# New orders and PSUM banks for a hand-planned attention and feed-forward kernel, with w1 loaded ahead of the first masks

## The chip, the cores and the metric

The kernel runs on one core of one Trainium2 chip. The metric is the device time of one execution in microseconds (us). It is given as the median over several executions, and beside it stands one execution taken with the hardware profiler, whose trace the quoted views come from.

## The reference

Attention with 16 extra keys ("beacons") that every query sees, and a causal mask behind them; its output goes through a two-layer network with the quick gelu.

```python
# q, k, v: (8, 8, 576, 64); beacon_k, beacon_v: (8, 8, 16, 64); w_in: (512, 2048); w_out: (2048, 512)
k_all = concatenate([beacon_k, k], axis=2)
v_all = concatenate([beacon_v, v], axis=2)
scores = (q @ k_all^T) / sqrt(64)
causal[:, 16:] = triu(ones((576, 576)), k=1)          # beacons are never masked
a = softmax(where(causal, -1e9, scores))
x = (a @ v_all), transposed to 4608 tokens x 512
h = x @ w_in
out = (h * sigmoid(1.702 * h)) @ w_out                # (4608, 512) float32
```

## The kernel before

**A plan written out.** The kernel first makes a list of some 1,740 operations. Each is made by `plan.op(...)` and numbered in the order of making; it knows its engine, an estimated duration and the operations that it depends on. Nothing is searched when the kernel is built: `ORDER` gives, for each engine, the numbers of its operations in the order in which the engine runs them (PE is TensorE, ACT ScalarE, DVE VectorE, POOL GpSimd, SP SyncE, Q the landing of transfers). `BANK` gives, for each PSUM tile in the order of the tiles' making, the PSUM bank (0 to 7) that it takes. `Plan.run` walks the lists and works out a planned start for each operation from the estimated durations. It then emits all operations sorted by planned start. Each engine runs its own instructions strictly in this order and waits at the head of its queue. What an operation waits for at run time is its data, and for the first operation on a PSUM tile also the last reader of the tile that had the bank before.

```python
todo = {e: [self.ops[i] for i in reversed(seq)] for e, seq in ORDER.items()}
keys = list(dict.fromkeys(o.ring for o in self.ops if o.ring is not None))
given = dict(zip(keys, BANK))
...
order.sort(key=lambda o: (o.start, o.seq))
```

**Attention.** The work comes in 16 sets, one for each half (four heads) of a batch row. Each set has two loads for k and q on GpSimd's queue (`ldqk`, line 452), turns of both on VectorE (`turn`, L519, with a small turn of the beacons' keys, L512, cast by `bk`, L508), scores on TensorE (`qk`, L586, later sets L575), exponentials on ScalarE (`exp`, L599, `E<-s`), causal masks on GpSimd (`mask`, L607, `E<-E`), and sums over keys on TensorE (`av`, L665). `av` with x = 2 gives the column sums of the exponentials (`u<-E,ones`), x = 0 and 1 the sums with v. VectorE takes the column sums' reciprocals (`z1` and `z2`, L675 to L686) and multiplies by them (`norm`, L703), which leaves x, transposed, in `xT` and frees the PSUM bank of the sums. In the later sets VectorE adds the key blocks up first (`zadd`, L625, `zs<-zs,E`), so that there are fewer products for the column sums.

**The feed-forward part.** The tokens come in ten groups. Groups 0 and 1 have 256 tokens each. For them a product `m1` (L727) takes two column blocks of w_in, ScalarE makes a tanh (L742), VectorE the gate (`gate`, L761), which frees the bank, and `m2` (L773) the second product. Groups 2 to 9 have 512 tokens. From group 3 on the first product runs partly in a form with fewer multiplications (`f` operations, L932, with sums of tokens and weights on VectorE, `sum22` and `sum21` at L951, and copies between banks on ScalarE, L942), and from group 2 on the second one too (`m2.g.p.n`, L845, whose results VectorE joins into `osb` with L861). The gelu of those groups is one ScalarE operation (L957). Stores go out on SyncE (L869, L876), the very last one on ScalarE's queue.

**Around the change.** The loads of w_in, `w1`, are eight: two row halves for each fourth of the columns, numbers 25 and 27 (columns 0 to 511), 33 and 35, 37 and 39 (columns 1024 to 1535), 41 and 43. They stand in GpSimd's queue with the masks: GpSimd has to issue each load itself, L489. The masks of the first set are 107, then 114 and 115 (their exponential is 113), those of the second 132 (exponential 131), then 135 and 136. Products m1.0.0 (151, 152), m1.0.2 (155, 156), m1.0.4 (159), m1.0.6 (162), m1.0.8 (165), m1.0.10 (168) and m1.0.12 (171) follow each other through the columns of w1; their tanhs are 153, 157, 160, 163 and on, their gates 154, 158, 161, 164 and on. Other names used below: 230 and 231 are the turns of k and q of the third set (229 is its beacons' cast); 124 and 125 are z1 and z2 of the first set's second half, 127 and 129 two of its norms; 144 is av1.2.1, the column sums of the second set's second half; 712 and 716 are the sums of f4.2; 833, 834, 835 and 885, 886, 887 are column-sum adds of sets 8 and 9.

In the last group the last product is made in two halves. The join of the first is 1731 with the store 1732 (128 KB, SyncE). The second half has two joins, 1736 with the store 1737 (64 KB, SyncE) and 1739 with the store 1740 (64 KB, ScalarE's queue).

**Idle-time products.** While TensorE waits early in the kernel, it is given products on a scrap tile whose results nobody reads (L1536). `FIRST` is the planned time in ns at which they begin; `until` is the end of the operation before. A unit is a product of 256 columns in 16 bits; the large sizes are made with 32-bit operands, 64 columns a unit.

```python
FIRST, WARM, COLS = 3800, 20000, 256
...
held, until = [None] * RING, FIRST
...
n = int((2.0 if until > FIRST else 1.8) * (o.start - max(until, since + 200)) / COLS)
```

Of the kernel before, what the change touches and what calls it, by code (L numbers as in the profile page):

```python
# [17 lines left out]
        76, 77, 90, 92, 116, 97, 98, 100, 101, 121, 103, 105, 137, 108, 110, 119, 142, 140, 112, 155, 151, 152,  # L18
        156, 130, 159, 123, 133, 162, 128, 232, 126, 144, 147, 149, 237, 165, 168, 239, 171, 191, 242, 246, 174,
        194, 263, 200, 197, 203, 206, 272, 253, 209, 212, 251, 274, 281, 258, 256, 249, 284, 277, 177, 222, 223,  # L20
        178, 288, 286, 413, 291, 293, 179, 184, 416, 224, 185, 186, 419, 225, 187, 180, 426, 327, 315, 317, 305,
        303, 319, 321, 325, 309, 307, 311, 329, 299, 301, 323, 313, 339, 348, 435, 444, 215, 340, 216, 217, 218,
        447, 349, 341, 350, 342, 359, 473, 360, 361, 364, 365, 351, 366, 615, 369, 367, 370, 371, 362, 618, 372,
        438, 483, 442, 440, 624, 383, 384, 488, 490, 643, 486, 385, 386, 376, 500, 645, 377, 502, 504, 378, 379,
        516, 532, 522, 538, 506, 534, 508, 536, 509, 512, 540, 541, 518, 520, 544, 550, 524, 554, 525, 552, 528,
        548, 564, 565, 573, 648, 634, 589, 566, 567, 590, 574, 575, 576, 813, 594, 584, 585, 586, 595, 816, 587,
        591, 592, 596, 657, 819, 637, 641, 639, 662, 827, 664, 660, 601, 597, 602, 845, 603, 604, 608, 670, 609,
        848, 610, 611, 674, 676, 879, 678, 672, 679, 682, 686, 708, 702, 692, 724, 706, 704, 720, 710, 711, 718,
        690, 714, 688, 734, 694, 695, 743, 836, 698, 722, 744, 735, 1017, 889, 841, 736, 754, 745, 737, 755,
        746, 1020, 839, 843, 894, 896, 892, 1027, 759, 760, 771, 756, 772, 1046, 757, 761, 764, 765, 773, 1048,  # L30
        762, 766, 767, 774, 902, 1051, 778, 906, 779, 904, 780, 781, 918, 911, 908, 934, 910, 952, 922, 920,
        938, 936, 924, 914, 926, 927, 940, 943, 942, 930, 966, 954, 950, 946, 956, 967, 1060, 1037, 1216, 986,
        968, 975, 976, 969, 977, 978, 987, 1219, 988, 989, 1040, 1063, 1042, 1222, 1067, 1065, 1044, 991, 1230,
        1073, 992, 993, 994, 996, 1248, 997, 998, 1003, 1004, 999, 1251, 1005, 1077, 1006, 1010, 1011, 1282,
        1075, 1012, 1082, 1081, 1013, 1089, 1079, 1105, 1121, 1091, 1093, 1107, 1109, 1085, 1125, 1097, 1095,
        1114, 1111, 1098, 1113, 1123, 1101, 1292, 1239, 1127, 1117, 1137, 1138, 1146, 1428, 1139, 1147, 1140,
        1148, 1149, 1242, 1246, 1431, 1244, 1299, 1295, 1297, 1438, 1162, 1157, 1158, 1163, 1167, 1457, 1168,
        1169, 1174, 1159, 1160, 1175, 1459, 1164, 1165, 1305, 1170, 1176, 1462, 1307, 1181, 1182, 1183, 1177,
        1321, 1311, 1309, 1337, 1184, 1325, 1323, 1313, 1327, 1314, 1339, 1329, 1317, 1353, 1330, 1341, 1333,
        1448, 1471, 1357, 1359, 1355, 1346, 1361, 1345, 1343, 1362, 1365, 1451, 1453, 1455, 1476, 1474, 1478,  # L40
        1349, 1377, 1378, 1484, 1386, 1500, 1379, 1387, 1380, 1486, 1504, 1388, 1402, 1502, 1516, 1403, 1508,
        1506, 1509, 1397, 1398, 1389, 1399, 1404, 1488, 1512, 1490, 1518, 1492, 1405, 1520, 1400, 1493, 1496,
        1414, 1532, 1407, 1522, 1524, 1525, 1534, 1408, 1409, 1536, 1415, 1565, 1538, 1528, 1540, 1410, 1611,
        1416, 1541, 1417, 1544, 1421, 1422, 1556, 1423, 1627, 1566, 1424, 1557, 1558, 1613, 1629, 1567, 1576,
        1559, 1568, 1577, 1581, 1631, 1578, 1582, 1615, 1583, 1633, 1579, 1635, 1636, 1584, 1643, 1586, 1639,
        1587, 1588, 1649, 1647, 1645, 1589, 1619, 1652, 1651, 1620, 1617, 1600, 1659, 1601, 1602, 1603, 1623,
        1655, 1665, 1593, 1663, 1594, 1595, 1596, 1667, 1668, 1661, 1683, 1684, 1671, 1685, 1692, 1708, 1693,
        1694, 1686, 1703, 1695, 1704, 1713, 1709, 1710, 1711, 1705, 1706, 1714, 1715, 1716, 1717, 1722, 1723,
# [3 lines left out]
        3, 1, 78, 79, 91, 93, 99, 102, 104, 106, 109, 111, 113, 153, 131, 157, 134, 160, 163, 233, 238, 166,  # L52
        169, 240, 172, 243, 175, 192, 195, 264, 198, 201, 204, 207, 273, 210, 213, 275, 278, 414, 417, 420, 226,
        188, 428, 427, 181, 316, 328, 318, 320, 322, 326, 304, 310, 308, 330, 312, 306, 300, 302, 324, 314, 445,
        219, 448, 474, 475, 347, 616, 619, 625, 626, 644, 501, 646, 503, 533, 505, 507, 535, 539, 537, 511, 517,
        513, 523, 519, 521, 543, 515, 551, 547, 555, 545, 527, 531, 529, 553, 549, 649, 572, 814, 817, 820, 828,
        829, 846, 671, 849, 675, 677, 880, 881, 681, 683, 703, 685, 673, 709, 707, 725, 705, 687, 693, 713, 717,
        691, 719, 721, 715, 689, 697, 701, 699, 723, 1018, 742, 1021, 1028, 1029, 1047, 1049, 903, 1052, 907,
        905, 919, 909, 935, 953, 913, 921, 923, 917, 925, 939, 915, 941, 929, 937, 933, 931, 949, 955, 945, 947,
        951, 957, 1217, 974, 1220, 1223, 1232, 1231, 1249, 1074, 1252, 1078, 1283, 1284, 1076, 1090, 1106, 1080,  # L60
        1092, 1122, 1084, 1094, 1086, 1110, 1126, 1096, 1108, 1112, 1088, 1100, 1104, 1124, 1120, 1116, 1102,
        1128, 1118, 1429, 1145, 1432, 1439, 1440, 1458, 1460, 1306, 1463, 1308, 1322, 1310, 1312, 1338, 1324,
        1326, 1328, 1340, 1316, 1318, 1320, 1354, 1332, 1342, 1334, 1358, 1360, 1356, 1336, 1344, 1364, 1352,
        1350, 1348, 1366, 1485, 1501, 1368, 1487, 1385, 1505, 1503, 1507, 1511, 1515, 1517, 1489, 1491, 1519,
        1513, 1521, 1495, 1497, 1533, 1523, 1535, 1499, 1531, 1537, 1539, 1527, 1529, 1547, 1545, 1543, 1612,
        1628, 1614, 1564, 1632, 1630, 1634, 1638, 1644, 1640, 1616, 1650, 1648, 1642, 1646, 1658, 1618, 1654,
        1660, 1626, 1622, 1656, 1664, 1666, 1624, 1662, 1672, 1674, 1670, 1691, 1740,
    ],
    "DVE": [
        73, 74, 75, 96, 94, 80, 95, 117, 118, 122, 138, 139, 120, 85, 143, 141, 231, 154, 229, 230, 124, 125,  # L70
        158, 129, 161, 127, 260, 164, 145, 146, 148, 150, 167, 170, 261, 173, 262, 247, 193, 176, 248, 196, 199,
        202, 205, 254, 208, 255, 211, 252, 214, 282, 259, 250, 423, 257, 410, 283, 411, 285, 412, 289, 287, 290,
        294, 425, 292, 424, 431, 432, 433, 492, 493, 295, 494, 434, 296, 333, 337, 472, 297, 331, 621, 335, 470,
        471, 343, 332, 334, 336, 344, 338, 436, 437, 298, 352, 353, 345, 479, 622, 623, 356, 346, 480, 355, 481,
        363, 482, 368, 439, 373, 484, 485, 354, 443, 441, 489, 491, 487, 496, 387, 497, 498, 499, 495, 380, 630,
        510, 631, 542, 514, 632, 546, 653, 526, 530, 556, 557, 560, 633, 568, 559, 577, 561, 569, 563, 558, 571,
        635, 562, 570, 581, 636, 654, 579, 655, 580, 656, 588, 593, 658, 659, 638, 640, 663, 642, 661, 578, 598,
        665, 666, 667, 668, 605, 669, 612, 832, 680, 833, 834, 684, 835, 885, 712, 716, 886, 887, 726, 730, 696,
        700, 837, 888, 838, 738, 747, 727, 731, 739, 890, 729, 728, 732, 842, 733, 891, 751, 840, 741, 844, 740,
        895, 897, 893, 749, 898, 1033, 748, 750, 758, 1034, 899, 763, 768, 1035, 900, 775, 901, 782, 912, 916,  # L80
        1056, 1057, 928, 1058, 932, 1036, 948, 944, 959, 958, 962, 970, 1059, 963, 960, 971, 1038, 964, 961,
        1039, 965, 1061, 973, 972, 1062, 983, 979, 980, 990, 1064, 1041, 1043, 1068, 1045, 1066, 1069, 981, 982,
        1070, 1235, 995, 1071, 1000, 1236, 1007, 1072, 1014, 1288, 1289, 1083, 1237, 1238, 1290, 1291, 1087,
        1099, 1103, 1119, 1115, 1240, 1241, 1293, 1130, 1134, 1142, 1294, 1132, 1136, 1131, 1129, 1135, 1133,
        1144, 1243, 1154, 1141, 1247, 1151, 1150, 1245, 1296, 1143, 1300, 1152, 1298, 1301, 1444, 1445, 1302,
# [1487 lines left out]
```

## Time and profile before

| | us |
| --- | --- |
| executions without the profiler | 318.36, 320.02, 318.30 |
| their median | 318.36 |
| the profiled execution | 319.39 |
| its span, first to last instruction | 317.6 |

| engine | busy us | share of the span |
| --- | --- | --- |
| TensorE, products | 309.3 | 97% |
| TensorE, weight loads (beside the products) | 232.4 | 73% |
| VectorE | 252.2 | 79% |
| ScalarE | 232.5 | 73% |
| GpSimd | 133.3 | 42% |

The granted TensorE clock is 1.00. In the trace PE stands for the products, PEld for weight loads, DVE for VectorE, ACT for ScalarE, POOL for GpSimd, SP for SyncE, `SPq`, `ACTq` and `POOLq` for their transfers. A timeline row has the start in us, the duration, the engine, the line, the instruction with its output and inputs, and a count of like instructions that are shown as one row; in square brackets stands the idle time before it and what ended that. A row of the waits has who waited for whom, the total in us, the number of waits, and the longest of them in us. A row of a chain has the start, the duration and the number of instructions. In the row of 40 digits each digit is a fortieth of the span, 9 meaning 90% busy or more. A row of the transfers has the size of one and the median time from issue to landing.

### The profile page before, as it was taken

How to read it: one execution, taken by the hardware profiler on the slowest of the kernel's cores; microseconds unless marked ns; L12 is line 12 of the kernel's file. 1: busy time of each engine (PE TensorE's matmuls, PEld its weight loads, DVE VectorE, ACT ScalarE, POOL GpSimd, SP SyncE). 2: the span in 40 equal slices, each digit the busy share in tenths (PEclk: the TensorE clock that was granted, in tenths of full speed). 3: DMA queues.
4: the chain of work that ended last, by engine and by line, in shares of the span. 5: the costliest groups of instructions: out<-in, count | busy, mean ns of one | idle time of the engine just before them, and what ended most of it. 6: DMA issues, size and time to landing. Idle time of an engine off the chain costs nothing. (4 is left out here: it accounts for less than half of the span.)

```text
span 317.6 us, 9341 instructions
## 1 busy us (share of the span) xinstructions
PE 309.3 (97%) x3964; PEld 232.4 (73%) x3964; DVE 252.2 (79%) x491; ACT 232.5 (73%) x309; POOL 133.3 (42%) x186
## 2 busy tenths in 40 slices
PE   6999999999999999989999999999999999999995
PEld 2677775445777777767778777877788888888884
DVE  4678888399998778888996998779977994595673
ACT  1688883796768987699869986898779668646630
POOL 8469765992785703593066406740321000000000
PEclk9999999999999999999999999999999999999999
DMA  7999999999799976699096943997012001020213
GB/s 116 179 187 134 170 182 204 173 185 123 74 154 125 194 57 103 84 179 167 2 96 68 158 122 67 135 165 71 3 35 99 4 1 35 33 69 0 101 56 111
DMA packets 112522, 33.51 MB, mean 106 GB/s; under 512 B 97504, under 2 KB 109920, under 8 KB 112480
## 3 DMA queue, kind: packets, MB, share of 16 engines
q0 software_dynamic: 83008, 18.55, 65.7%
q1 hardware_dynamic: 29264, 14.28, 19.7%
q8 instruction: 31, 0.51, 0.7%
q14 instruction: 11, 0.09, 0.1%
q10 hardware_dynamic: 208, 0.07, 0.1%
HBM read 37.22 MB, written 14.22 MB: 162 GB/s over the span
## 5 line engine op out<-in xcount | busy, mean ns | idle before, releaser
L599 ACT ACTIVATE E<-s 128x2048 f16<-128x2048 f32 (+3 forms) x59 | 90.6, 1552 | 30.8 <-PE s L586 15.4
L607 POOL TENSOR_SCALAR_AFFINE_SELECT E<-E 128x512 f16<-128x512 f16 (+2 forms) x78 | 58.8, 836 | 102.6 <-ACT E L599 85.8
L845 PEld LDWEIGHTS <-g 128*128 128x128 f16 x768 | 73.3, 98 | 11.9 <-issue 0.9
L845 PE MATMUL u<-w,g 128*128 128x256 f16 x512 | 66.5, 273 | 0.0
L957 ACT ACTIVATE g<-u 128x512 f16<-128x512 f32 x96 | 54.3, 620 | 13.6 <-PE u L932 7.6
L861 DVE SCALAR_TENSOR_TENSOR osb<-u,osb 128x512 f32<-128x512 f32 (+2 forms) x51 | 33.2, 655 | 17.8 <-PE u L845 17.2
L727 PE MATMUL u<-xT,w 128*128 128x256 f16 (+1 forms) x256 | 45.9, 326 | 1.4 <-DMA w<-in_moe_w_in_dram 0.9
L932 PEld LDWEIGHTS <-SF 128*128 128x128 f16 x384 | 37.2, 98 | 7.6 <-issue 0.4
L932 PE MATMUL u<-sig,SF 128*128 128x256 f16 x288 | 41.2, 272 | 0.0
L727 PEld LDWEIGHTS <-w 128*128 128x128 f16 x256 | 24.1, 98 | 16.0 <-issue 1.4
L468 POOL DMA_DIRECT2D vb<-in_v_dram x32 | 35.4, 1154 | 0.0
L845 PE MATMUL u<-tB,g 128*128 128x256 f16 x256 | 35.2, 273 | 0.0
L942 ACT ACTIVATE u<-u 128x512 f32<-128x512 f32 x48 | 28.4, 596 | 5.6 <-PE u L932 3.7
L932 PEld LDWEIGHTS <-w 128*128 128x128 f16 x288 | 27.9, 98 | 5.0 <-issue 1.1
L703 DVE TENSOR_TENSOR xT<-u,rz 128x352 f16<-128x352 f32 (+6 forms) x58 | 26.3, 481 | 4.2 <-PE u L665 3.9
L932 PE MATMUL u<-xT,w 128*128 128x256 f16 x192 | 28.3, 272 | 0.3
L665 PE MATMUL u<-E,vb 128*32 128x352 f16 (+8 forms) x928 | 27.4, 262 | 0.1
L793 DVE TENSOR_TENSOR g<-g 128x512 f16<-128x512 f16 x64 | 26.1, 428 | 0.7
L625 DVE TENSOR_TENSOR zs<-zs,E 128x1344 f16<-128x1344 f16 (+2 forms) x36 | 23.7, 664 | 1.5 <-POOL E L607 0.5
L665 PEld LDWEIGHTS <-vb 128*32 128x32 f16 (+1 forms) x928 | 20.3, 96 | 6.0 <-issue 2.5
L951 DVE TENSOR_TENSOR u<-u,kn 128x512 f32<-128x512 f32 x24 | 16.1, 693 | 9.0 <-PE u L932 4.8
L951 DVE TENSOR_TENSOR u<-u,qn 128x512 f32<-128x512 f32 x24 | 16.2, 695 | 6.2 <-PE u L932 5.5
(72 smaller groups left out, 446.2 us busy)
## 6 DMA issues: line engine op xcount, KB each, us to landing
out_dram<-osb SPq DMA_DIRECT2D x35, 256.0 KB, 3.5
vb<-in_v_dram POOLq DMA_DIRECT2D x24, 128.0 KB, 6.1
kn<-in_k_dram POOLq DMA_DIRECT2D x8, 288.0 KB, 6.8
qn<-in_q_dram POOLq DMA_DIRECT2D x8, 288.0 KB, 7.0
qD<-in_q_dram POOLq DMA_DIRECT2D x8, 288.0 KB, 7.1
kD<-in_k_dram POOLq DMA_DIRECT2D x8, 288.0 KB, 7.3
w<-in_moe_w_in_dram POOLq DMA_DIRECT2D x8, 256.0 KB, 7.2
w<-in_moe_w_out_dram POOLq DMA_DIRECT2D x4, 512.0 KB, 10.4
```

The source lines that it names most:

```text
L468: nc.gpsimd.dma_start(out=t[0 : hi - lo, j, h0:h1, :], in_=v[b, h0:h1, lo:hi, :].rearrange("h n d -> n h d"),)
L599: nc.scalar.activation(out=Es[s][:, h0:h1, c0:c1], in_=sall[(i, p)][:, :, o : o + c1 - c0], func=AFT.Exp, scale=0.125,)
L607: nc.gpsimd.affine_select(out=blk, in_=blk, compare_op=ALU.is_ge, fill=0.0, base=a - s0s[j] + (Nb if j == 0 else 0), pattern=[[0, Q], [1, w]],
L665: nc.tensor.matmul(u[32 * h : 32 * h + 32, a:e], lhs, src[0:kw, h, col : col + e - a], start=first, stop=last, skip_group_check=s >= EARLY ...
L703: nc.vector.tensor_tensor(out=xT[:, 2 * hs + x : 2 * hs + x + n, at : at + c1 - c0], in0=rings[("av", s, x, half)][:, 0 : n * w].rearrange ...
L727: nc.tensor.matmul(u[:, o + a - t0 : o + e - t0], w1t[:, kp, nt * P : (nt + 1) * P], xT[:, kp, a % XR : (e - 1) % XR + 1], start=(kp == 0 ...
L845: nc.tensor.matmul(u[:, HM * mt : HM * (mt + 1)], lhs[:, n, mt * P : (mt + 1) * P], rhs[:, n, :], start=(n == 0 and (mt == 0 or apart) and ...
L861: nc.vector.scalar_tensor_tensor(out=osbs[(g, dst)][:, c0:c1], in0=rings[("p", g, p)][:, c0:c1], scalar=scale_of(g), in1=osbs[(g, src)][:, ...
L932: nc.tensor.matmul(u[:, HM * n : HM * (n + 1)], lhs[x][:, (2 * i + n) * P : (2 * i + n + 1) * P], rhs[:, x, :], start=fresh and n == 0 and ...
L942: nc.scalar.mul(out=ring_tile(dst)[:, :], in_=rings[src][:, :], mul=1.0)
L951: nc.vector.tensor_tensor(out=rings[dst][:, :], in0=rings[src][:, :], in1=p7s[(g, i)], op=ALU.add)
L957: nc.scalar.activation(out=gts[g][:, n : n + 2, HM * h : HM * (h + 1)], in_=rings[src][:, :].rearrange("p (n w) -> p n w", n=2), func=AFT. ...
```

## The change

All lists of `ORDER` hold the same numbers in another order, `BANK` gives other banks, and `FIRST` is 4600 instead of 3800. The operations, their durations and their dependencies stay as they are. On GpSimd, w1 load 37 now stands ahead of masks 114 and 115, and 41 and 43 ahead of mask 132. On VectorE, gate 158 and column sums 124 have moved ahead of the turn 230; on ScalarE, tanh 153 stands ahead of exponential 113, and 157 ahead of 131. Tile av1.2.1 takes the bank that m1.0.4 had. Later in the kernel most lists have neighbours changed over, GpSimd's loads of the later sets further apart. At the end, store 1737 stands ahead of 1732, and join 1736 ahead of 1739. The diff, cut to the places named:

```diff
     "PE": [
-        76, 77, 90, 92, 116, 97, 98, 100, 101, 121, 103, 105, 137, 108, 110, 119, 142, 140, 112, 155, 151, 152,
-        156, 130, 159, 123, 133, 162, 128, 232, 126, 144, 147, 149, 237, 165, 168, 239, 171, 191, 242, 246, 174,
+        76, 77, 90, 92, 116, 97, 98, 100, 101, 119, 121, 103, 137, 105, 140, 142, 108, 110, 151, 155, 152, 112,
+        156, 162, 130, 159, 123, 133, 128, 126, 232, 144, 149, 147, 237, 165, 168, 239, 171, 174, 242, 246, 197,
...
     "ACT": [
-        3, 1, 78, 79, 91, 93, 99, 102, 104, 106, 109, 111, 113, 153, 131, 157, 134, 160, 163, 233, 238, 166,
+        3, 1, 78, 79, 91, 93, 99, 102, 104, 106, 109, 111, 153, 113, 157, 131, 134, 160, 163, 233, 238, 166,
...
     "DVE": [
-        73, 74, 75, 96, 94, 80, 95, 117, 118, 122, 138, 139, 120, 85, 143, 141, 231, 154, 229, 230, 124, 125,
-        158, 129, 161, 127, 260, 164, 145, 146, 148, 150, 167, 170, 261, 173, 262, 247, 193, 176, 248, 196, 199,
+        73, 74, 75, 96, 94, 85, 95, 80, 117, 118, 120, 122, 138, 139, 141, 143, 154, 231, 158, 229, 124, 230,
+        125, 127, 161, 164, 145, 146, 150, 410, 260, 148, 129, 167, 170, 261, 247, 423, 173, 262, 176, 193, 248,
...
-        665, 666, 667, 668, 605, 669, 612, 832, 680, 833, 834, 684, 835, 885, 712, 716, 886, 887, 726, 730, 696,
+        666, 598, 667, 668, 605, 669, 832, 612, 680, 684, 885, 833, 834, 886, 887, 835, 712, 716, 888, 726, 696,
...
-        1718, 1719, 1726, 1731, 1739, 1736,
+        1718, 1719, 1726, 1731, 1736, 1739,
     ],
     "POOL": [
-        8, 10, 16, 14, 12, 17, 21, 19, 23, 25, 27, 51, 33, 35, 49, 107, 31, 29, 39, 115, 114, 41, 37, 61, 132,
-        43, 136, 135, 53, 55, 65, 63, 71, 390, 235, 236, 234, 67, 69, 241, 245, 857, 45, 392, 47, 244, 57, 394,
+        8, 10, 14, 12, 16, 17, 19, 21, 23, 25, 33, 27, 35, 51, 31, 49, 107, 29, 39, 37, 114, 115, 41, 43, 53,
+        67, 132, 135, 136, 61, 234, 55, 236, 69, 63, 235, 65, 71, 390, 392, 45, 47, 57, 241, 394, 245, 244, 265,
...
     "SP": [
-        1591, 1574, 1605, 1598, 1701, 1720, 1727, 1732, 1737,
+        1574, 1591, 1598, 1605, 1701, 1720, 1727, 1737, 1732,
     ],
...
-    FIRST, WARM, COLS = 3800, 20000, 256
+    FIRST, WARM, COLS = 4600, 20000, 256
```

180 rows, old and new, of tables (BANK, ORDER) are left out of this document.

## The prediction

> **What bounds the kernel now.** I read the page's busy times first, then the waits, the end of the chain, the windows by stage, and last the timelines of the stages in which the change reorders work.
>
> ```profile
> PE 309.3 (97%) x3964; PEld 232.4 (73%) x3964; DVE 252.2 (79%) x491; ACT 232.5 (73%) x309; POOL 133.3 (42%) x186
> PE   6999999999999999989999999999999999999995
> ...
> PEld L575 <- issue: 3.8, 18, 0.2
> PE u L727 <- DMA w<-in_moe_w_in_dram: 0.9, 2, 0.6
> ...
> 302.69 11.37 PE u L845 x104
> ...
> 100.00:110.00 10.00, 9.89 (x93) 8.01 (x84) 7.69 (x13) 9.94 (x17) 6.99 (x8) 1.00 1.73 206
> 110.00:135.00 25.00, 24.89 (x353) 18.21 (x352) 21.16 (x49) 19.16 (x22) 7.64 (x11) 1.00 0.75 85
> 135.00:144.00 9.00, 8.20 (x73) 6.26 (x72) 8.02 (x8) 8.97 (x13) 9.00 (x13) 1.00 1.90 188
> 144.00:200.00 56.00, 56.00 (x730) 42.59 (x730) 49.07 (x95) 46.33 (x60) 23.35 (x32) 1.00 0.88 95
> 200.00:250.00 50.00, 49.87 (x610) 39.50 (x610) 40.73 (x78) 43.76 (x63) 14.01 (x22) 1.00 0.58 77
> ```
>
> TensorE is busy for 309.3 of 317.6 us, no other engine for more than 79%, and the chain ends with 104 products in a row. So the time is TensorE's work plus its holes. The holes come to 317.6 − 309.3 = 8.3 us. In the windows from 100 to 250 us (columns: TensorE, its weight loads, VectorE, ScalarE, GpSimd, then granted clock) the holes of TensorE are 0.11, 0.11, 0.80, 0.00 and 0.13 us. In the waits, TensorE's two waits on the w1 loads are 0.9 us. The rest of the 8.3 us lies at the two ends, as the first and last digits of its row show (6 and 5 where all between but one are 9). The diff moves instructions and renames PSUM banks; it adds and removes no arithmetic except five units of idle-time products. An edit can therefore do three things only: close or open a hole, lengthen the start or the tail, or change how often TensorE changes its kind of product.
>
> The profiled execution took 319.39 us: the span of 317.6 and 1.79 around it. The median of the three runs is 318.36, 1.03 lower. I make the sum as a difference to the span and apply it to both.
>
> **Part 1: the w1 loads ahead of the masks.** GpSimd issues these loads and makes the masks, in one queue.
>
> ```profile
> 19.36 0.70 POOL L489 DMA_DIRECT2D w<-in_moe_w_in_dram  x1
> 21.25 1.06 POOL L607 TENSOR_SCALAR_AFFINE_SELECT E<-E 128x320 f16<-128x320 f16 x2 [1.19 <-ACT E L599]
> 22.26 1.43 POOL L489 DMA_DIRECT2D w<-in_moe_w_in_dram  x2
> ...
> 24.24 0.49 POOL L607 TENSOR_SCALAR_AFFINE_SELECT E<-E 128x320 f16<-128x320 f16 x1
> 24.66 0.73 POOL L489 DMA_DIRECT2D w<-in_moe_w_in_dram  x1
> ```
>
> ```profile
> 26.62 0.67 PE L665 MATMUL u<-E,ones 128*32 128x288 f16 x20
> 27.12 1.17 PE L665 MATMUL u<-E,vb 128*32 128x288 f16 x40
> 28.29 0.53 PE L586 MATMUL s<-qT,kT 32*128 32x288 f16 x16
> 29.08 1.92 PE L727 MATMUL u<-xT,w 128*128 128x256 f16 x16 [0.27 <-DMA w<-in_moe_w_in_dram]
> ...
> 32.42 1.70 PE L727 MATMUL u<-xT,w 128*128 128x256 f16 x14 [0.65 <-DMA w<-in_moe_w_in_dram]
> ```
>
> GpSimd stood idle for 1.19 us ahead of masks 115 and 114, while load 37 was second of the two behind them (22.98, i.e. 22.26 plus half of 1.43). After the change 37 goes into that idle time, at 20.06, 2.9 us earlier. It costs the masks nothing as long as it ends (20.06 + 0.72) before the mask's data come (21.25). Loads 41 and 43 pass mask 132 and the beacon load 61: 43 moves from 24.66 to about 23.7. TensorE's products m1.0.8 waited 0.27 us on 37, and m1.0.12 waited 0.65 us on 43. Lost waiting: 0.27 + 0.65 = 0.92. I take all of it, **−0.92** (bounds 0, if other loads hold the queues, and −0.92).
>
> What moves back in that queue: mask 132 comes behind 41, 43 and two loads of k and v (53, 67), so about 25.1 instead of 24.24; masks 135 and 136 stay where they were (25.6), and their readers are the products at 26.62 and 27.12. Those readers get no earlier, as part 2 shows, so I put 0 here; without that cover it would be the 0.9 us of mask 132.
>
> **Part 2: VectorE's order at 20 to 28 us.** In PE's list the sums av1.2.1 (144, the row at 26.62) take a new bank. Before, it was the bank that norm 129 frees; after, it is bank 2, whose tile before was m1.0.4, freed by its gate 161.
>
> ```profile
> 19.73 1.45 ACT L599 ACTIVATE E<-s 128x1536 f16<-128x1536 f32 x1 [0.94 <-PE s L586]
> 21.07 0.59 ACT L742 ACTIVATE sig<-u 128x512 f16<-128x512 f32 x1
> ...
> 22.53 0.21 DVE L512 STREAM_TRANSPOSE kT<-bkn 128x32 f32<-128x32 f32 x1
> 22.77 1.26 DVE L519 STREAM_TRANSPOSE kT<-kn 128x576 f32<-128x576 f32 x1
> 23.88 0.44 DVE L675 STREAM_TRANSPOSE zt<-u 128x288 f32<-128x288 f32 x1
> ...
> 25.00 0.65 DVE L761 SCALAR_TENSOR_TENSOR g<-sig,u 128x512 f16<-128x512 f16 x1
> 25.63 0.46 DVE L703 TENSOR_TENSOR xT<-u,rz 128x288 f16<-128x288 f32 x1
> 26.01 0.69 DVE L761 SCALAR_TENSOR_TENSOR g<-sig,u 128x512 f16<-128x512 f16 x1
> ```
>
> Before, 161 is the row at 26.01. It runs behind 230 (the turn of k, two rows, from 22.53), the column sums 124 and 125 (from 23.88), gate 158 (25.00) and norm 129 (25.63). After, the list is 154, 231, 158, 229, 124, 230, 125, 127, 161. I let 124 start no earlier than before, as its column sums come from TensorE no earlier; from 23.88 the queue ahead of 161 is 124 and 125 (25.00 − 23.88 = 1.12), 230 (23.88 − 22.53 = 1.35) and 127, a norm like 129 (0.46): 23.88 + 2.93 = 26.81. Gate 161 is 0.8 us later and ends at 26.81 + 0.69 = 27.50. Then 144 can start, instead of at 26.62: 27.50 − 26.62 = **+0.9**, all of it on TensorE, which runs its list in order. Bounds: 0 (if 124's data are there earlier, or TensorE is behind by as much for another reason) and +1.5 (exp 113 and tanh 153 change places, so exp 113 and its masks come 0.59 later, and this adds up).
>
> **Part 3: the middle.** Between 28 and 300 us the lists swap neighbours nearly everywhere. The windows above say what that can bring: holes of 1.15 us in all from 100 to 250. The one place where I see an added queue is VectorE at 143 to 148.
>
> ```profile
> 143.10 1.11 DVE L625 TENSOR_TENSOR zs<-E 128x1856 f16<-128x1856 f16 x1
> ...
> 145.36 1.30 DVE L951 TENSOR_TENSOR u<-u,qn 128x512 f32<-128x512 f32 x2 [1.15 <-PE u L932]
> 146.57 1.47 DVE L625 TENSOR_TENSOR zs<-zs,E 128x1344 f16<-128x1344 f16 x2
> ```
>
> Before, VectorE waited 1.15 us and made the two sums of f4.2 (712, 716), then the two adds of column sums (886, 887). After, 886, 887 and 835 stand ahead of 712, and they want GpSimd's masks, which in that list move too. 1.15 us of idle time takes most of the 1.47; 0.32 is left, so **+0.3** (bounds 0, if TensorE has other work queued, and +1.1, if a mask is late by the 0.8 us which GpSimd, busy for 9.00 of 9.00 from 135 to 144, hasn't to spare). All other swaps I put at 0, with ±1.0: down for the 1.15 us of holes, up by the like.
>
> TensorE changes its kind of product three times more often (141 for 138 in its list). "PEld L575 <- issue" gives 3.8 us over 18 waits, 0.2 each; most changes show none, so I take 0.1 each, **+0.3** (0.0 to 0.6).
>
> **Part 4: the tail.**
>
> ```profile
> out_dram<-osb SPq DMA_DIRECT2D x1, 128.0 KB, 1.9
> ...
> out_dram<-osb ACTq DMA_DIRECT2D x1, 64.0 KB, 1.7
> ...
> 313.66 1.28 SPq L876 DMA_DIRECT2D out_dram<-osb  x2
> ...
> 314.08 0.49 DVE L861 SCALAR_TENSOR_TENSOR osb<-u,osb 128x128 f32<-128x128 f32 x2 [0.45 <-PE u L845]
> 314.40 0.37 ACTq L876 DMA_DIRECT2D out_dram<-osb  x1
> ```
>
> Before, SyncE issued the 128 KB store 1732 at 313.66 and the 64 KB store 1737 behind it, from joins 1731 and 1736; join 1739 and its store on ScalarE's queue stood beside them. After, 1737 stands ahead of 1732, and 1736 ahead of 1739. 1737 can't be issued before 1736 has run (one half of the row at 314.08), so at about 314.4; 1732 follows a store's issue of 0.37 to 0.64 later, at about 314.8, and lands 1.9 later, at 316.7. Before, the last to land were the two small stores, 314.4 + 1.7 to 1.9, about 316.3. So **+0.4** (bounds 0 and +0.8).
>
> **Part 5: five units fewer of idle-time products.**
>
> ```profile
> 2.60 5.30 PE L1536 MATMUL u<-tB 128*128 128x512 f32 x7 [2.60 <-DVE tB L370]
> 7.74 0.68 PE L549 MATMUL p<-low,eye 128*128 128x112 f16 x12
> ...
> 9.66 1.34 PE L1536 MATMUL u<-tB 128*128 128x512 f32 x3
> ```
>
> ```profile
> 6.25 1.26 DVE L519 STREAM_TRANSPOSE kT<-kn 128x576 f32<-128x576 f32 x1 [2.27 <-DMA kn<-in_k_dram]
> ```
>
> The first row is the burst that fills the time until the first products on data, at 7.74, which want kT, turned at 6.25 + 1.26 = 7.51. It has 26 units (the 1.8 × 3700 / 256 of its formula), 5.30 / 26 = 0.20 us each; five fewer end it about 1.0 earlier, at 6.9, before kT is there. So the cut is worth 0, hidden by the wait for kT, with 7.51 − 7.74 = −0.2 as the other bound. But the 7 records took 0.76 each and the 3 at 9.66, of the same kind, 0.45 each: the array is slower in the first microseconds. If a shorter burst makes the fast state come later, the products at 7.74 (0.68) and a score like them run slow: 2 × 0.68 × (0.76 − 0.45) / 0.45 = +0.9. I take 0, since 4.3 us of the burst stay, and keep +0.9 as a rival. [...]
>
> **Sum.** −0.9 + 0.9 + 0.3 + 0.3 + 0.4 + 0 = +1.0: a span of 318.6, a profiled execution of 320.4, and a median of **319.3**.
>
> **Rivals.** A measurement of this kernel tells some 0.5% from no change, 1.6 us: the bounds are 316.8 and 320.0.
> *Faster: the waits go and nothing takes their place.* 161's delay does not show (124's data come early, since tanh 153 now runs first), VectorE's idle 1.15 us swallows the adds, and the middle's holes shrink. That gives −0.92, −1.15 in the middle and +0.4: −1.7, so 316.7. For it: the holes are real, and swaps over the whole list can close them. Against it: each is small, the middle's largest (0.80 of 9.00) sits where ScalarE is busy for 8.97 and GpSimd for 9.00, which no order shortens.
> *Slower: late masks for the zadds at 140 to 148 us.* VectorE's 886 and 887 at the head of the queue wait for GpSimd's masks, which are busy throughout, so 712 and 716 and the bank that they free are late by a mask's time, and TensorE has nothing else. A mask there that is one place later costs the 0.8 to 1.1 us above; with the rest of the sum (+1.0 − 0.3) that is +1.7, 320.1, and with part 2's upper bound 320.7. It decides if 886's mask ends after 146.0. For it: the window at 135 already has holes of 0.80. Against: the 56.00 of 56.00 of the next window, where TensorE had work enough ahead.
> *The clock rival*, +0.9 on the sum: 320.3.
> *The change doesn't do what it says:* w1's loads are issued earlier, but land when they did, because the queues are full: the 0.92 stays but is covered by the 0.9 of part 2, which then holds TensorE while the loads land: 319.3 too. In the forecast the gain and the delay cancel; here neither shows.
>
> **Chances and range.** Forecast with its neighbours, including the last rival (316.8 to 320.0): 0.38. Faster: 0.25. Slower by the masks, the clock or part 2's upper bound: 0.37. Of the faster cases nearly all lie just below 316.8, as −1.7 needs all holes at once; of the slower ones, part 2's +1.5, part 3's +1.1 and the clock's +0.9 together would pass 321.5. The range is 316.8 to 321.5, with the likeliest case's own at 318.3 to 320.0.
>
> **What would show it.** Part 1: no w1 line in TensorE's waits, load 37 at about 20.1. Part 2: gate 161 at about 26.8, and a hole ahead of the L665 products at 26.6 named for it. Part 3: a hole in 135 to 150 that grows by 0.3. Part 4: SyncE's last store at 314.8, 128 KB, and the span's end 2.3 us behind the last join. Part 5: the first scores still at 7.74 or up to 0.2 earlier, and 0.68 long. Wrong would be: a hole of over 0.5 us in another place, or holes of under 0.2 us from 100 to 250.

## The result and the profile after

The kernel after takes 321.27 us (median of 6 executions, 320.90 to 321.58); the kernel before, run beside it, 319.16 (6 executions, 318.30 to 320.02). The ratio is 1.007 with a 95% interval of 1.005 to 1.0089: slower by 0.7%, 2.1 us. The profiled execution took 321.42, its span is 319.7, 2.1 longer than before's 317.6.

TensorE in stages, the kernel after (columns: stretch, its length, then busy time of TensorE, weight loads, VectorE, ScalarE, GpSimd; granted clock, share of the transfers, GB/s):

```profile
20.00:28.00 8.00, 6.36 (x174) 5.10 (x172) 6.62 (x12) 7.24 (x8) 6.22 (x11) 1.00 1.31 175
28.00:40.00 12.00, 11.50 (x211) 9.29 (x203) 10.46 (x22) 9.46 (x12) 10.79 (x17) 1.00 1.46 154
...
110.00:135.00 25.00, 24.75 (x345) 17.87 (x345) 21.43 (x48) 19.34 (x22) 9.54 (x14) 1.00 1.09 124
135.00:144.00 9.00, 7.88 (x78) 6.07 (x75) 7.44 (x9) 8.57 (x12) 8.25 (x12) 1.00 1.12 157
144.00:200.00 56.00, 54.96 (x715) 41.48 (x714) 46.11 (x93) 45.65 (x61) 23.65 (x28) 1.00 1.11 111
200.00:250.00 50.00, 50.00 (x597) 39.97 (x595) 41.83 (x79) 44.38 (x61) 16.86 (x25) 1.00 0.45 71
```

The rows of before for the two first stretches, which the prediction did not show:

```profile
20.00:28.00 8.00, 8.00 (x210) 6.30 (x211) 6.94 (x15) 7.57 (x8) 6.62 (x13) 1.00 1.34 154
28.00:40.00 12.00, 10.99 (x180) 8.60 (x169) 9.10 (x17) 10.01 (x13) 10.28 (x17) 1.00 1.48 155
```

The holes (length less busy) grew from 0.00 to 1.64 us at 20 to 28, and from 0.00 to 1.04 at 144 to 200. They fell from 1.01 to 0.50 at 28 to 40, where the waits on w1 were, and from 0.13 to 0.00 at 200 to 250. At 135 to 144 they went from 0.80 to 1.12. So there are two new holes, one where the prediction put it and one where it put nothing.

Holes alone don't give the difference, because in the first 20 us idle-time products fill them and count as busy. The rows of those products alone, before and then after:

```profile
12.00:20.00 8.00, 1.46 (x6) 0.32 (x5) 1.00 1.25 201
```

```profile
12.00:20.00 8.00, 0.39 (x1) 0.10 (x1) 1.00 1.28 192
```

Both windows read 8.00 busy of 8.00, but before has 1.46 us of filling there and after only 0.39: the new order gains 1.07 us in a stretch that looked full. A ledger that leaves the filling out compares the traces at equal work. Each product is found in both traces by its operation; work is the sum of the planned durations of the operations done. The table gives the time of before, and by how much each kernel stands later (+) or earlier at the same work. The first products on data do not start at the same time in each execution (at 7.47 to 8.30 us in the nine profiled ones with the longer burst, at 6.58 to 7.02 in the five with the shorter), and the rows from 25 us of work on contain what is left of that. How much that can be, three kernels with the same first 185 us show: at 25 us of work b_w1 stands at -0.26, c_late at +0.64 and c_late2 at -0.69. So the steps between rows are read here, and not the single values.

```
work   before   after   a_join782  a_joins  a_bank144  a_first   b_w1
   2    13.00   -0.12     -0.66     -0.63     -0.60     +0.03    +0.29
   6    19.41   -1.07     -1.60     -1.58     -1.54     -0.92    +0.30
  16    31.17   +1.08     +0.64     +1.09     +0.88     +1.23    +0.26
  25    42.12   +0.09     -0.34     +0.10     -0.11     +0.25    -0.26
 110   134.03   +0.54     +0.20     +0.54     +0.34     +0.71    -0.28
 120   145.74   +0.90     +0.56     +0.54     +0.33     +1.07    -0.28
 145   172.51   +0.67     +0.34     +0.33     +0.12     +0.85    -0.29
 150   177.51   +2.31     +0.68     +0.67     +0.46     +2.49    -0.29
 281   313.92   +1.79     +0.15     +0.15     -0.07     +1.98    -0.30
```

Read down the column "after": 1.0 us gained by 19 us, 2.15 lost by 31, 1.0 gained back by 42 (0.8 of it where the second wait on w1 was), 0.5 lost in small steps by 134, 0.36 lost at 140, 0.2 gained by 172, 1.64 lost at 174, and 0.5 gained later; the tail adds 0.3. The early part comes out even, as far as one execution of each can tell. What makes the kernel slower is the middle, above all one place at 174 us.

There, TensorE, ScalarE and VectorE in the kernel after:

```profile
175.01 0.60 PE L932 MATMUL u<-xT,w 128*128 128x256 f16 x4 [0.76 <-ACT u L942]
```

```profile
172.58 0.60 ACT L957 ACTIVATE g<-u 128x512 f16<-128x512 f32 x1
174.38 1.07 ACT L942 ACTIVATE u<-u 128x512 f32<-128x512 f32 x2 [1.20 <-DVE osb L861]
```

```profile
171.41 0.83 DVE L793 TENSOR_TENSOR sig<-xT 128x512 f16<-128x512 f16 x1
172.17 1.49 DVE L625 TENSOR_TENSOR zs<-E 128x1856 f16<-128x1856 f16 x1
173.59 0.68 DVE L861 SCALAR_TENSOR_TENSOR osb<-u,osb 128x512 f32<-128x512 f32 x1
```

The row at 173.59 is join 782. Its product had ended at 171.64, but VectorE's list has the column-sum add 1056 of set 11 (172.17) ahead of it. Join 782 frees the bank that ScalarE's copy 919 takes (first of the two at 174.38). ScalarE, which runs in order, stood 1.20 us for it, and TensorE's product at 175.01 depends on that copy. In before the copy follows the same join in its bank (there bank 3, in after bank 0). What differs for this join is VectorE's order. In before 782 stands ahead of 1056, so the join ran at 171.44, the copy at 172.89 and the add at 175.24:

```profile
171.44 0.69 DVE L861 SCALAR_TENSOR_TENSOR osb<-u,osb 128x512 f32<-128x512 f32 x1 [0.89 <-PE u L845]
...
175.24 1.12 DVE L625 TENSOR_TENSOR zs<-E 128x1856 f16<-128x1856 f16 x1
```

```profile
172.89 0.59 ACT L942 ACTIVATE u<-u 128x512 f32<-128x512 f32 x1
```

The early holes are these rows of TensorE, and the gate that the second one names is the first of two in VectorE's row:

```profile
25.81 0.64 PE L586 MATMUL s<-qT,kT 32*128 32x288 f16 x24 [0.44 <-ACT E L599]
27.45 0.68 PE L665 MATMUL u<-E,ones 128*32 128x288 f16 x20 [0.99 <-DVE g L761]
...
31.05 1.03 PE L727 MATMUL u<-xT,w 128*128 128x256 f16 x8 [0.50 <-DVE xT L703]
```

```profile
26.71 1.28 DVE L761 SCALAR_TENSOR_TENSOR g<-sig,u 128x512 f16<-128x512 f16 x2
```

### The profile page after: what moved, and what is told of

Same layout as the page of the kernel before. It is cut to its first block, busy times and chain, and to the rows that moved or that the text cites. A ratio compares the mean times of both kernels' runs of the same rounds, so it can differ in the third digit from the quotient of the medians.

```text
span 319.7 us, 9317 instructions
## 1 busy us (share of the span) xinstructions
PE 308.5 (96%) x3959; PEld 232.9 (73%) x3959; DVE 251.8 (79%) x491; ACT 232.5 (73%) x309; POOL 135.8 (42%) x186
## 4 chain that ended last, share of the span: by engine, by line
PE 60%; ACT 4%; DVE 4%; issue 2%; DVEq 0%; ACTq 0%
PE u L845 27%; PE u L932 19%; PE u L665 6%; PE u L727 4%; PE s L575 4%; DVE zs L625 2%; DVE osb L861 1%; ACT E L599 1%; ACT u L942 1%; ACT g L957 1%; ACT L957 1%; DVE sig L793 1%; PE s L586 1%; DVE xT L703 0%; DVE rz L686 0%
## 5 line engine op out<-in xcount | busy, mean ns | idle before, releaser
L607 POOL TENSOR_SCALAR_AFFINE_SELECT E<-E 128x512 f16<-128x512 f16 (+2 forms) x78 | 61.1, 816 | 82.5 <-ACT E L599 71.0
L468 POOL DMA_DIRECT2D vb<-in_v_dram x32 | 33.8, 1125 | 16.1 <-PE u L665 15.4
L665 PE MATMUL u<-E,vb 128*32 128x352 f16 (+8 forms) x928 | 27.5, 263 | 0.3 <-DVE xT L703 0.2
L665 PEld LDWEIGHTS <-vb 128*32 128x32 f16 (+1 forms) x928 | 20.3, 96 | 6.8 <-issue 3.5
```

What stands on the lines that cost most here:

```text
L468: nc.gpsimd.dma_start(out=t[0 : hi - lo, j, h0:h1, :], in_=v[b, h0:h1, lo:hi, :].rearrange("h n d -> n h d"),)
L607: nc.gpsimd.affine_select(out=blk, in_=blk, compare_op=ALU.is_ge, fill=0.0, base=a - s0s[j] + (Nb if j == 0 else 0), pattern=[[0, Q], [1, w]],
L665: nc.tensor.matmul(u[32 * h : 32 * h + 32, a:e], lhs, src[0:kw, h, col : col + e - a], start=first, stop=last, skip_group_check=s >= EARLY ...
```

## The experiments

In the kernels below the written-out lists are broken differently into lines, so all later lines have numbers lower by two (the join is L859, the add L623). Diffs name the operations. Each median stands beside the kernel before run on the same chip (its medians there: 319.42, 319.65 and 319.39).

**a_join782**: one pair of VectorE's list.

```diff
 "DVE" of the kernel after:
-  ... 1033, 775, 901, 1056, 782, 1057 ...
+  ... 1033, 775, 901, 782, 1056, 1057 ...
```

> The kernel after, with one pair of VectorE's list changed over: the join 782 ahead of the column-sum add 1056. Theory 1 (a late join holds a bank): 782 had its data at 171.64 and ran at 173.59 behind 1056, so the ScalarE copy 919, which takes 782's bank, waited 1.20 us, and TensorE stood for 0.93 us at 174 and 0.7 in three smaller holes behind it. With 782 at 172.2, 919 can run right behind ScalarE's gelu at 173.2 and 1.2 us comes back: about 320.1 where the kernel after has 321.3. Rival (ScalarE's copies in that stage are late anyway, the bank is only the last of several waits): less than 0.4 us comes back, 320.9 or more.

Measured: 320.19 us, ratio to before 1.002 (1.0005 to 1.0035), 1.1 us under the kernel after. The stage is full again, and the join runs at 171.83:

```profile
144.00:200.00 56.00, 55.94 (x727) 42.69 (x726) 46.93 (x94) 46.85 (x62) 22.52 (x27) 1.00 1.26 116
...
171.83 0.68 DVE L859 SCALAR_TENSOR_TENSOR osb<-u,osb 128x512 f32<-128x512 f32 x1
```

In the ledger the step at 145 to 150 shrinks from 1.64 to 0.34: half of the change's loss, or a little more, is this pair. The rival is out.

**a_bank**: VectorE's list as in the kernel after, the banks passed round.

```diff
 BANK of the kernel after:
-  f5.1 "b" (919): 0    f5.0 "f" (908): 3    f5.1 "f" (924): 7
+  f5.1 "b" (919): 3    f5.0 "f" (908): 7    f5.1 "f" (924): 0
```

> The kernel after, VectorE's list untouched, but with three banks passed round: the copy 919 takes bank 3 (free since 171.5) instead of bank 0, product f5.0.7 (908) bank 7, and f5.1.7 (924) bank 0. Theory 1 (order and bank together make the hole): 919 no longer waits for join 782, 1.2 us comes back as with the changed order, about 320.1. Rival (what costs is that VectorE is late, not the bank): the sums 912 and 916 stay late and under 0.4 us comes back.

Measured: 319.99 us, ratio 1.0024 (1.0003 to 1.0044). VectorE still makes the join late, at 173.42, and nothing waits for it: ScalarE's copies run without a gap, and the ledger's step at 145 to 150 is 0.34 here too.

```profile
172.01 1.50 DVE L623 TENSOR_TENSOR zs<-E 128x1856 f16<-128x1856 f16 x1
173.42 0.68 DVE L859 SCALAR_TENSOR_TENSOR osb<-u,osb 128x512 f32<-128x512 f32 x1
```

```profile
172.41 0.60 ACT L955 ACTIVATE g<-u 128x512 f16<-128x512 f32 x1
172.91 1.08 ACT L940 ACTIVATE u<-u 128x512 f32<-128x512 f32 x2
```

So it is neither order nor bank alone: here the late join costs 1.30 us (1.64 − 0.34) where the next tile has been given its bank, and nothing that shows where it has not.

**a_joins**: the same for join 612 as well, at 136 us.

```diff
 "DVE" of a_join782:
-  ... 669, 832, 612, 680 ...
+  ... 669, 612, 832, 680 ...
```

> The kernel after with join 782 ahead of add 1056, as before, and the join 612 ahead of the add 832 too. Theory (the same mechanism at 137 us, smaller): 612 ran 0.4 us after its data, which moved ScalarE's copy 675, and TensorE stood 0.3 us longer there; 0.3 us faster than with 782 alone, 319.9. Rival (that stage is bound by GpSimd's masks and ScalarE, so the hole only moves): no change against 782 alone, 320.2.

Measured: 319.49 us, ratio 0.9998 (0.9978 to 1.0019). The stretch from 135 to 144 gets its 0.3 us back (7.88 to 8.19), and the step of 0.36 at 110 to 120 in the ledger goes to 0.00. By the medians, taken on two chips, the second pair brings 0.7; the traces show the 0.36.

```profile
135.00:144.00 9.00, 8.19 (x81) 6.32 (x78) 7.64 (x9) 8.85 (x13) 9.00 (x12) 1.00 1.07 158
```

With these two pairs changed the kernel after is as fast as the kernel before.

**b_w1**: the w1 loads alone, in the kernel before.

```diff
 "POOL" of the kernel before:
-  ... 29, 39, 115, 114, 41, 37, 61, 132, 43, 136, 135 ...
+  ... 29, 39, 37, 115, 114, 41, 43, 61, 132, 136, 135 ...
```

> The kernel before, with nothing changed but GpSimd's list: w1 load 37 ahead of masks 115 and 114, loads 41 and 43 right behind those, ahead of load 61 and mask 132. Theory (the two waits of 0.27 and 0.65 us on w1 are on the path, and nothing takes their place): 0.9 us faster than the kernel before, 318.3 against 319.2. Rival (the loads only change places in the transfers' queues, or others become late): within 0.2 us of the kernel before.

Measured: 318.83 us, ratio 0.9971 (0.9955 to 0.9988): 0.9 us faster by the ratio, 0.6 by the medians. It beats both kernels. No row of TensorE's waits names w1 any more; the stretch from 28 to 40 is fuller by 0.63 us than in before. Not all of the 0.92 comes back. Two pauses of TensorE's weight loads, for which the profile has no cause ("issue"), stand beside it: with them two rows of 16 products take 2.22 and 2.19 us, where a like row takes 1.92.

```profile
28.00:40.00 12.00, 11.62 (x194) 9.14 (x183) 9.48 (x19) 10.55 (x13) 11.14 (x18) 1.00 1.41 153
...
30.45 0.53 PEld L725 LDWEIGHTS <-w 128*128 128x128 f16 x5 [0.31 <-issue]
...
35.45 0.64 PEld L725 LDWEIGHTS <-w 128*128 128x128 f16 x6 [0.28 <-issue]
```

**a_first**: `FIRST = 3800` in the kernel after.

> The kernel after with FIRST at 3800 again, five units of idle-time products more. Theory (the first scores wait for the turns, which end at 8.9, so the length of the burst is hidden): within 0.2 us of the kernel after, 321.3; the masked start at 7.0 goes back to 7.7 and runs in 0.7 us instead of 1.2, and the scores behind it stay at 9.0. Rival (TensorE reaches its fast state later after the shorter burst, and that costs on the path): 0.5 to 0.9 us faster than the kernel after.

Measured: 321.66 us, 0.1% above the kernel after (ratio to before 1.0064, 1.0044 to 1.0084): no difference. The first products in the kernel after, and then here:

```profile
7.02 1.16 PE L549 MATMUL p<-low,eye 128*128 128x112 f16 x12
...
8.97 0.64 PE L586 MATMUL p<-qT,kT 32*128 32x288 f16 x24
```

```profile
7.76 0.68 PE L547 MATMUL p<-low,eye 128*128 128x112 f16 x12
...
9.12 0.64 PE L584 MATMUL p<-qT,kT 32*128 32x288 f16 x24
```

In the kernel after the same 12 products take 1.16 us instead of 0.68: in this execution TensorE is still slower behind the shorter burst. The scores behind them could have begun when the turn of q had ended, at 8.52 (the row below, of the kernel after). They began 0.45 later, behind the slow products and the idle-time products that follow them; in a_join782, with the same burst and fast products (0.68), they began at 8.42, after TensorE had stood 0.43 us for the turn. In a_first, with fast products too, they began at 9.12. So a_first shows that the whole does not get faster with the longer burst, and not that the slower products were hidden.

```profile
7.26 1.26 DVE L519 STREAM_TRANSPOSE qT<-qn 128x576 f32<-128x576 f32 x1
```

**a_early and a_early2**: before's orders, banks and burst up to 42 us in the kernel after.

```diff
 for each engine: the first n of before's list, then the rest of after's
+  n: PE 51, ACT 34, DVE 57, POOL 39, Q 29; SP 6 (a_early) or 21 (a_early2); FIRST = 3800
```

> The kernel after, with all engines' orders, banks and the idle-time products of the first 42 us from the kernel before. Theory (what the new early part gains, a start 1 us further on by 17 us and no wait on w1, it gives back behind gate 161 and the masks): the early parts are worth the same within 0.4 us, so 320.9 to 321.4. Rival (the prediction's sum, in which the early part costs the tail's share and more): 0.8 us or more faster than the kernel after. Rival on the other side (w1 ahead is a net gain in the kernel after): 0.5 us or more slower.

> The early part of before in the kernel after once more, now with SyncE's list from before up to 85 us too. (In the first try the loads of the beacons' keys stood in after's order on SyncE, behind a memset that before's VectorE list makes late: the cast 229 came 2.8 us late, and TensorE stood 2.27 us at 25 us.) Theory: the early parts of both kernels are worth the same within 0.4 us, so 320.9 to 321.4. Rival 1 (the early part costs the kernel after 0.8 us or more): 320.5 or less. Rival 2 (w1 ahead is a net gain in the kernel after): 321.8 or more.

Measured: 330.79 us (ratio 1.0348, 1.0294 to 1.0402) and 325.06 (1.0197, 1.0148 to 1.0246). Neither answers its question: the seam makes new waits. In a_early, TensorE stood 2.27 us at 25 us for the late beacon loads. In both, behind the seam a tile is given the bank of a tile just made, and TensorE waits for its gate and norm (a_early2):

```profile
42.49 1.91 PE L725 MATMUL u<-xT,w 128*128 128x256 f16 x16 [1.16 <-DVE g L759]
47.35 0.41 PE L663 MATMUL u<-E,ones 128*32 128x288 f16 x12 [1.17 <-DVE g L759]
48.70 0.41 PE L663 MATMUL u<-E,vb 128*32 128x288 f16 x12 [0.94 <-DVE xT L701]
```

That the early parts come out even rests on the ledger alone.

**a_best2**: a_early2 with w1 ahead, both joins, and before's end.

> The same with the three w1 loads moved ahead, the joins 782 and 612 ahead of the adds, and the last joins and stores in the order of before. If the parts add up: 321.3 less 0.2, 0.6 to 0.9 (w1 alone measured 0.3% or 0.9 us), 1.8 (both joins, measured) and 0.3 (end) gives 318.1 to 318.4, 1 us faster than the kernel before. If they overlap: 318.8, as with w1 alone, or slower.

Measured: 323.21 us (ratio 1.0132, 1.0093 to 1.0172), 1.85 under a_early2: the seam is in it, so the sum was not tested. The first try, a_best, had a_early's seam and gave 329.43 us:

> The same early part of before in the kernel after, with the three w1 loads moved ahead in it, the joins 782 and 612 ahead of the adds, and the joins and stores at the end in the order of before. The parts add up if they are independent: -0.2 (early part), -0.9 (w1), -1.1 (782), -0.3 (612), -0.3 (end) from 321.3 give 318.5, which is 0.9 us faster than the kernel before. If the gains overlap: no faster than the kernel before with w1 moved.

**c_late and c_late2**: before with w1 ahead, and after's lists of TensorE, ScalarE and VectorE and its banks from 185 us on; in c_late2 one join further ahead.

```diff
 "DVE" of c_late:
-  ... 1171, 1446, 1447, 1467, 1178, 1468 ...
+  ... 1171, 1446, 1178, 1447, 1467, 1468 ...
```

> The kernel before with the three w1 loads moved ahead, and from 185 us on the orders of TensorE, ScalarE and VectorE and the banks of the kernel after (GpSimd's and SyncE's lists stay, and so does the order of the last joins). By the traces the kernel after gains 0.7 us between 185 and 260 us on the kernel before. Theory (that gain is in these three lists): 1.6 us faster than the kernel before, 317.7. Rival (it comes from GpSimd's masks and SyncE's transposes, which stay, or is only the other side of the hole at 174): 0.9 us faster, as with w1 alone, or less.

> The kernel before with w1 ahead and after's late lists, with one change against the first try: the join 1178 ahead of the add 1447. In the first try 1447 waited 3.95 us for GpSimd's mask at the head of VectorE's list, join 1178 (data at 236.7) ran at 240.3, the copy 1310 that takes its bank waited 2.18 us, and TensorE 1.91. Theory (join behind an add that waits for a mask, a third time): 1.9 to 2.2 us faster than the first try, 318.7 to 319.0. Rival (the masks are late for the sums of that stage as well): under 1 us back, 320 or more.

Measured: 320.92 us (ratio 1.0046, 1.0023 to 1.0069) and 320.10 (1.0033, 1.0008 to 1.0058). Neither brings after's late gain to the kernel before. In c_late the hole at 240 us is the pattern of 174 once more: an add waits for a mask at the head of VectorE's list, the join behind it is late, ScalarE waits for the bank, TensorE for ScalarE.

```profile
239.04 0.33 DVE L623 TENSOR_TENSOR zs<-zs,E 128x320 f16<-128x320 f16 x1 [3.95 <-POOL E L605]
...
240.32 0.68 DVE L859 SCALAR_TENSOR_TENSOR osb<-u,osb 128x512 f32<-128x512 f32 x1
```

```profile
241.04 0.58 ACT L940 ACTIVATE u<-u 128x512 f32<-128x512 f32 x1 [2.18 <-DVE osb L859]
```

```profile
241.67 1.03 PE L930 MATMUL u<-sig,SF 128*128 128x256 f16 x8 [1.91 <-ACT u L940]
```

Moving the join brought 0.8 us of the 1.9 to 2.2 expected, because the next join, 1185, stands behind the same adds (239.96 in c_late2) and holds the next copy:

```profile
240.68 0.58 ACT L940 ACTIVATE u<-u 128x512 f32<-128x512 f32 x1 [2.04 <-DVE osb L859]
```

**a_bank144**: a_joins, with the end of before, and two banks changed over.

```diff
 BANK:   -  av1.2.1 (144): 2   av1.1.1 (149): 3
         +  av1.2.1 (144): 3   av1.1.1 (149): 2
 "DVE":  -  ... 1731, 1736, 1739     "SP":  -  ... 1737, 1732
         +  ... 1731, 1739, 1736            +  ... 1732, 1737
```

> The kernel after with both joins ahead of the adds, the last joins and stores in the order of before, and the banks of av1.2.1 (144) and av1.1.1 (149) changed over, so that 144 takes the bank that norm 127 frees (26.80) and not that of gate 161 (27.39). Theory of part 2 (144 waits for the bank): the hole of 0.99 us at 27.45 shrinks to 0.5, and the products behind move up by as much; with 0.3 us at the end this gives 318.7 against 319.5. Rival (masks 135 and 136 and the norms hold the stage, the bank is only the last of them): the hole stays over 0.8, and only the 0.3 us at the end come back, 319.2.

Measured: 319.33 us (ratio 1.000, 0.998 to 1.0021), 0.2 under a_joins. The hole ahead of 144 goes from 0.99 to 0.42 us, but the products behind it then wait for norms:

```profile
26.70 0.68 PE L663 MATMUL u<-E,ones 128*32 128x288 f16 x20 [0.42 <-DVE xT L701]
...
29.61 1.03 PE L725 MATMUL u<-xT,w 128*128 128x256 f16 x8 [0.59 <-DVE xT L701]
30.84 1.03 PE L725 MATMUL u<-xT,w 128*128 128x256 f16 x8 [0.20 <-DVE xT L701]
```

By 25 us of work it stands 0.2 ahead of a_joins. So of the 0.99 us the bank was worth 0.2; the rest comes back as waits for VectorE's norms, that is, for the same queue at another instruction. In this stage both theories hold a part.

## Why the prediction was right or wrong

The time lay in the range, on the side of the forecast and further out: 2.1 us were lost where 1.0 was forecast. By the prediction's own sign of being wrong, a hole of over 0.5 us in another place, its account of the middle was wrong: that hole is the 0.76 at 175.01. Point by point:

**Part 1, w1: right.** Load 37 was forecast at about 20.1 and left at 19.6 (the second of the two at 18.95); no w1 row is left in the waits. Alone the move is worth 0.6 to 0.9 us.

```profile
18.95 1.39 POOL L489 DMA_DIRECT2D w<-in_moe_w_in_dram  x2
```

**Part 2, VectorE at 20 to 28: the place and the size right, the bank overrated.** Gate 161 was forecast at 26.81 and ran at 26.71; 144 at 27.50 and ran at 27.45, behind a hole of 0.99 named for the gate. Two holes beside it, 0.44 ahead of the score at 25.81 and 0.50 at 31.05, were not in the sum, nor was the gain of 1.07 us that idle-time products hid at 12 to 20. That these cancel, within what one execution of each can tell, is luck.

**Part 3, the middle: the step that failed.** From 42 us to the last product the ledger grows by 1.7 us (+0.09 to +1.79), where 0.3 for the adds and 0.3 for the kinds of product were forecast. The adds 886, 887 and 835 ahead of 712 cost next to nothing: VectorE had even 0.26 us to wait before 712 and 716.

```profile
141.62 4.38 DVE L625 TENSOR_TENSOR zs<-zs,E 128x1344 f16<-128x1344 f16 x5
146.26 1.30 DVE L951 TENSOR_TENSOR u<-u,qn 128x512 f32<-128x512 f32 x2 [0.26 <-PE u L932]
```

The +0.3 was there, but from 832 ahead of 612 nine us earlier. And the term "all other swaps 0, ±1.0" was mis-sized: it held 1056 ahead of 782, in a place that lost 1.64 us, and a_join782 and a_bank each bring back 1.30 of them. I had bounded the term by the holes of before. Holes bound what a new order can win, by my reckoning. What it lost here depended on what it put ahead of an instruction that frees a bank: how long that takes (1.49 us here) and how long it waits itself (3.95 in c_late). The stretch from 144 to 200, 56.00 of 56.00 busy, was read as safe, and it had no slack.

**Kinds of product, +0.3: not seen.** The row on which it rested is the same after the change, 3.8 us in 18 waits; no step of the ledger is named for it. The like row of the L665 products grew from 4.5 to 6.2 us, but a_joins, whose list for TensorE is that of the kernel after, is as fast as before (ratio 0.9998).

```profile
PEld L575 <- issue: 3.8, 18, 0.2
```

**Part 4, the tail: right.** 1737 and 1732 were issued as two at 316.19, the large store second; the span ends 0.3 us further behind the last product than before (3.9 for 3.6). +0.4 was forecast. With the end of before, in a_bank144, it is 3.5 again. The sign "2.3 us behind the last join" was misreckoned: it is 3.0 in before and 3.3 in after.

```profile
316.19 0.82 SPq L876 DMA_DIRECT2D out_dram<-osb  x2
```

**Part 5: the price right, the reason half wrong.** The masked products don't wait for kT: they ran at 7.02, as soon as the burst was over, and took 1.16 us, not 0.68. What waits for the turns are the scores behind them. The clock rival was right that the products behind the shorter burst can be slow: 1.16 us in the kernel after and 1.07 in a_bank, though 0.68 in three other executions. In the kernel after that cost 0.48 us on 12 products, and the first scores began 0.45 behind their turn. In the whole time nothing of it shows: a_first is no faster.

**The rivals.** The slower one was the right mechanism in kind, an add ahead of something that TensorE needs, but it put that ahead of 712 and on late masks, where it cost next to nothing; the adds that cost stood ahead of joins 612 and 782. The faster one failed since something did take the waits' place. The last one is out: no wait on w1 is left.

## What to carry to other kernels

When orders are rearranged, look for each long instruction that has moved ahead of one that frees a buffer, and ask who has been given that buffer next. Here the step at the late reader was 0.34 us where its bank was not the next one taken (a_bank) and 1.64 us where it was: ScalarE, which runs in order, stood 1.20 us for it and passed the delay on. Holes in the bound engine are a bound on what a new order can win, not on what it can lose: the stretch from 144 to 200 us had none (56.00 of 56.00), and it was there that 1.64 us were lost. Filling instructions count as busy (1.46 us of the 8.00 from 12 to 20 in before), so take them out before you call a stretch full.

## What the runs showed of the hardware

**The time at which TensorE's products get faster is not the same in each execution.** In the kernel after, a 32-bit product of 512 columns takes 1.06 us in the burst (the one at 4.46) and 0.70 at 9.54; the granted clock reads 1.00 for both. (The prediction's 0.76 and 0.45 are means in which 16-bit products count too.) The burst is the same instructions, yet it lasted 4.14 to 4.63 us in the five profiled executions with the shorter one and 5.04 to 5.92 in the nine with the longer. In two of the five the 12 products behind it were still slow (1.16 us in the kernel after, 1.07 in a_bank), in the other three not (0.68). The kernel after, and then a_join782:

```profile
2.59 4.63 PE L1536 MATMUL u<-tB 128*128 128x512 f32 x6 [2.59 <-DVE tB L370]
```

```profile
2.60 4.14 PE L1534 MATMUL u<-tB 128*128 128x512 f32 x6 [2.60 <-DVE tB L368]
6.58 0.68 PE L547 MATMUL p<-low,eye 128*128 128x112 f16 x12
```

**Behind a pause the granted clock fell in some executions.** In a_early, behind the hole of 2.27 us at 25 us, the granted clock of the next 6 us was 0.72, and the 20 products of a sum took 1.15 us (0.68 ahead of the change of clock). Behind the hole of 0.99 us in the kernel after it stayed at 1.00 (20 to 28 and 28 to 40 us), and so it did in a_early2 behind three of 1.16, 1.17 and 0.94 us (its rows above; 40 to 60 us). The same program does not always get the same clock: in the six executions of a_early2 its mean was 1.00 in four (324.70 to 325.21 us), 0.997 in one (325.25) and 0.993 in one (328.25). In all six of a_early it was 0.982 to 0.995. That the pause is the cause is a reading of these numbers; no run changed the pause alone.

```profile
28.00:34.00 6.00, 6.00 (x148) 4.81 (x141) 5.13 (x13) 2.55 (x2) 5.64 (x9) 0.72 1.10 147
```

```profile
27.85 0.68 PE L663 MATMUL u<-E,vb 128*32 128x288 f16 x20 [2.27 <-DVE zt L673]
...
29.18 1.15 PE L663 MATMUL u<-E,vb 128*32 128x288 f16 x20
```

**The kernel before scatters.** In one group of 29 executions it took 317.93 to 321.64 us; the six of the kernel after lie between 320.90 and 321.58. Of the 2.9 us between the median of 318.36, from which the prediction started, and 321.27, 0.8 is that its three executions lay low in that scatter. Why the two scatter differently was not tried.
